# Two batches interleaved at the head of a fused attention and maximum-layer kernel

## The chip, the cores and the metric

The kernel runs on one core of one Trainium2 chip. Its time is the device time of one execution in microseconds. TensorE (PE) multiplies, VectorE (DVE), ScalarE (ACT) and GpSimd (POOL) work on SBUF beside it, and the kernel issues all its DMAs from SyncE (SP). Each engine works through its own list of instructions in order and waits at an instruction until what it needs is there.

## What is computed

A packed attention for each of 8 batches and 8 heads (576 tokens, 64 wide): 32 packed queries p attend to the tokens' k and v, and then the tokens' q attend to the 32 results as keys and values. Behind it, over the 512 columns of all heads, stand two layers: the maximum of three products with 512 x 768 weights, and a product with W_out (768 x 512).

```python
def sm_attn(qq, kk, vv):
    s = scale * np.matmul(qq, kk.transpose(0, 1, 3, 2))
    s = s - np.max(s, axis=-1, keepdims=True)
    a = np.exp(s)
    a = a / (np.sum(a, axis=-1, keepdims=True) + 1e-09)
    return np.matmul(a, vv)
p_packed = sm_attn(p, k, v)
out = sm_attn(q, p_packed, p_packed)
...
h = np.maximum(np.maximum(x @ w1, x @ w2), x @ w3)
return (h @ w_out).astype(np.float32)
```

## The kernel before

**The weights** arrive as 64-bit floats; each of 18 tiles of the first layer (j = 0 to 5, c = 0 to 2; 128 x 512) and 6 of W_out is made 32-bit floats by `to_f32` (L97): two ACT steps (L108, L112), one DVE shift (L114) and one POOL add (L118). W_out's tiles are then split in a rounded part (hi) and a rest (lo), L90. Tiles of j = 0 and 1 land in the buffers with the tag "h", the others in four slots of `stage`.

**A batch.** `scores` (L184) multiplies the packed queries with k, takes the maximum on DVE and the exponential on ACT; `turn` (L219) transposes the result on PE; `values` (L238) multiplies with v; `packed` (L258) transposes the result into `pt_sb`. `att2` (L266) multiplies q with it, turns 32 x 32 blocks on DVE, subtracts the maximum on POOL, takes the exponential on ACT, normalizes and turns back on DVE, and splits the weights in hi (ACT) and lo (POOL): `a2h`, `a2l`. `pw_step` (L319) multiplies a weight tile column j with `pt_sb`, so that the layer needs only the 32 packed rows of each head, and splits the product in hi (ACT) and lo (DVE). `moe_in` (L373) forms for each j and half of the tokens (hf) three sums of six products (hi*hi, lo*hi, hi*lo for two groups of heads r) and takes their maximum on ACT and DVE (L399, L402); the hidden tile is split again. `moe_out` (L411) forms eight output blocks (m, hf), each of 6 x 3 products with W_out, copies them on ACT and sends them out on SP.

**The order.** Batch 0's attention is written out as one list (`FIRST`, L42). From then on PE follows a clock: each step of `moe_in` and `moe_out` is one tick (60 per batch), and `STAGES` says at which tick the stages of the next batch's attention and the projections begin; the other engines' order is left to the scheduler. Layer one of batch 0 takes its weights as they are converted (`CONVERT`, L55), layer two follows, and batch 1's attention lies in between these at ticks 10 to 46 (`STAGES_0`). Then comes batch 1, and so on.

PSUM has two double banks (`ps_big`: scores, turned weights, q's scores, projections) and four single ones (`ps_moe`: the layers' sums; batch 0's `turn`). k, v share four buffers (tag "kv"), hidden tiles seven (tag "h").

Of the kernel before, what the change touches and what calls it, by code (L numbers as in the profile page):

```python
# [10 lines left out]
F32 = mybir.dt.float32  # L11
# [11 lines left out]
P = 128  # L23
G = 2
# [37 lines left out]
def fused_kernel(ctx: ExitStack, tc: tile.TileContext, kp, qt, va, vb, wi, wo, out):  # L62

# [24 lines left out]
    stage = const.tile([P, NST * 2 * WC], F32, name="stage")  # L88

    def split(hi, lo, src, eng_hi, eng_lo):  # L90
        if eng_hi is nc.scalar:
            nc.scalar.copy(out=hi, in_=src)  # L92
        else:
            eng_hi.tensor_copy(out=hi, in_=src)
        eng_lo.tensor_tensor(out=lo, in0=src, in1=hi.bitcast(F32), op=ALU.subtract)  # L95

    def to_f32(dst, src, n):  # L97

        words = src.bitcast(U32).rearrange("p (n two) -> p n two", two=2)
        low, high = words[:, :, 0], words[:, :, 1]
        nc.scalar.activation(  # L108
            out=high.bitcast(F32), in_=high.bitcast(F32), func=AF.Prelu, scale=2.0 ** -111, alpha=-2.0 ** 32,
        )  # L110
        up = low.bitcast(I32)
        nc.scalar.activation(out=up, in_=low, func=AF.Copy, scale=2.0 ** -29)  # L112
        yield 1
        nc.vector.tensor_scalar(  # L114
            out=dst.bitcast(U32), in0=high, scalar1=3, scalar2=None, op0=ALU.logical_shift_left,
        )
        yield 1
        nc.gpsimd.tensor_tensor(out=dst.bitcast(I32), in0=dst.bitcast(I32), in1=up, op=ALU.add)  # L118

# [3 lines left out]
    staged = {}  # L123
    slot = [0]

    def next_slot():
        k = slot[0] % NST
        slot[0] += 1
        return stage[:, k * 2 * WC:(k + 1) * 2 * WC].bitcast(I64)

    def load_w_in(j, c):

        if j < 2:
            t = pool.tile([P, WC], I64, name=f"wi{j}_{c}", tag="h", bufs=NJ + 1)
# [5 lines left out]
    def conv(j, c):  # L140
        return to_f32(w_sb[:, j, c * WC:(c + 1) * WC], staged.pop((j, c)), WC)

    def run(stages):
        for _ in stages:
            pass

    def load_w_out(j):
        t = next_slot()
        nc.sync.dma_start(out=t, in_=wo[j])
        staged["o", j] = t  # L150

    def conv_out(j):
        f = pool.tile([P, DM], F32, name=f"wof{j}", tag="t", bufs=4)
        yield from to_f32(f, staged.pop(("o", j)), DM)
        yield 2
        split(wo_hi[:, j], wo_lo[:, j], f, nc.scalar, nc.gpsimd)

    loaded = {}
# [22 lines left out]

    s1, a1, a1t, av, r1, pp = {}, {}, {}, {}, {}, {}

    def scores(b):  # L184

        kt = [loaded.pop(("k", b, g)) for g in range(G)]
        s = [ps_big.tile([P, 2, 512], F32, name=f"s1_{b}_{r}", tag="big") for r in range(R)]
        for hf in range(2):
            for n, (g, pr) in enumerate(QUADS):
                for r in range(R):  # L190
                    o = slice(64 * r, 64 * r + 64)
                    w = 2 * S + 64 * pr + 32 * r
                    nc.tensor.matmul(  # L193
                        out=s[r][32 * n:32 * n + 32, hf, 0:HS],
                        lhsT=kt[g][o, w:w + NP],
                        rhs=kt[g][o, pr * S + hf * HS:pr * S + (hf + 1) * HS],
                        start=True, stop=True,
                    )
        yield 1
        mx = pool.tile([P, R], F32, name=f"mx{b}", tag="mx", bufs=2)  # L200
        nm = pool.tile([P, R], F32, name=f"nm{b}", tag="nm", bufs=2)
        z1 = pool.tile([P, R], F32, name=f"z1_{b}", tag="z1", bufs=2)
        r1[b] = pool.tile([P, R], F32, name=f"r1_{b}", tag="r1", bufs=2)
        for r in range(R):
            nc.vector.tensor_reduce(out=mx[:, r:r + 1], in_=s[r][:, :, 0:HS], axis=AX.XY, op=ALU.max)
# [12 lines left out]

    def turn(b, r):  # L219

# [6 lines left out]
        a = a1.pop((b, r))  # L227
# [10 lines left out]
    def values(b, rs):  # L238
# [25 lines left out]
    a2, last = {}, {}  # L264

    def att2(b):  # L266
        q = [loaded.pop(("q", b, g)) for g in range(G)]
        pt = pt_sb[b % 2]
        s2 = [ps_big.tile([P, 2, 512], F32, name=f"s2_{b}_{r}", tag="big") for r in range(R)]
        for hf in range(2):  # L270
            for n, (g, pr) in enumerate(QUADS):
                for r in range(R):
                    o = slice(64 * r, 64 * r + 64)
                    nc.tensor.matmul(  # L274
                        out=s2[r][32 * n:32 * n + 32, hf, 0:HS],
                        lhsT=pt[o, NP * n:NP * n + NP], rhs=q[g][o, pr, hf * HS:(hf + 1) * HS],
                        start=True, stop=True,
                    )
        yield 2

        e, e3, m2 = [], [], []
        for r in range(R):
            t = pool.tile([P, S], F32, name=f"e{b}_{r}", tag="t", bufs=4)
            for hf in range(2):
                nc.vector.transpose(out=t[:, hf * HS:(hf + 1) * HS], in_=s2[r][:, hf, 0:HS])
# [4 lines left out]
            nc.vector.tensor_reduce(out=m, in_=e3[r], axis=AX.X, op=ALU.max)  # L290
# [5 lines left out]
        for r in range(R):
            nc.scalar.activation(out=e[r], in_=e[r], func=AF.Exp, scale=SCALE)
            yield 1
        for r in range(R):
            z = pool.tile([P, NT], F32, name=f"z2_{b}_{r}", tag="z2", bufs=2)  # L300
            nc.vector.tensor_reduce(out=z, in_=e3[r], axis=AX.X, op=ALU.add)
            nc.vector.tensor_scalar_add(out=z, in0=z, scalar1=1e-9)
            nc.vector.reciprocal(out=z, in_=z)
            nc.vector.tensor_tensor(
                out=e3[r], in0=e3[r], in1=z.unsqueeze(2).to_broadcast([P, NT, NP]), op=ALU.mult,
            )
            yield 1
            et = pool.tile([P, S], F32, name=f"et{b}_{r}", tag="t", bufs=4)
            last["et"] = nc.vector.transpose(out=et, in_=e[r])
            yield 1  # L310
            hi = pool.tile([P, S], F32R, name=f"a2h{b}_{r}", tag="a2h", bufs=4)
            lo = pool.tile([P, S], F32R, name=f"a2l{b}_{r}", tag="a2l", bufs=4)
            split(hi, lo, et, nc.scalar, nc.gpsimd)
            a2[b, r] = (hi, lo)
            yield 1
# [3 lines left out]
    def pw_step(b, j):  # L319
# [256 lines left out]
```

## Time and profile before

| | us |
|---|---|
| median of three runs | 516.0 (515.9 to 517.64) |
| the profiled execution | 517.84 |
| its span | 516.1 |

The span is what the profile sees from the first instruction to the last; an execution lasts 1.74 longer. One execution was profiled. Rows of the profile name the line, the engine, the operation, what it writes and reads by the program's names, the count, the busy time, the mean of one in ns and the idle time of the engine ahead of it, with what ended that idle time. Matmuls overlap their successors, so the time between starts, not a matmul's duration, is what one costs; the chain of work, in which consecutive pieces are merged, gives it.

### The profile page before, as it was taken

Reading aid. Unit: us, or ns where it says so; the run is one execution under the profiler, and the core shown is the slowest. Engines: PE = TensorE matmul, PEld = TensorE weight load, DVE = VectorE, ACT = ScalarE, POOL = GpSimd, SP = SyncE. Lnnn points to the kernel's source line nnn. Section 1 sums busy time; section 2 is a strip of 40 time slices with the busy share of each in tenths; the row PEclk is TensorE's granted clock in tenths of the full one; section 3 lists DMA queues with packets and bytes.
Section 4 is the critical chain, followed back from the end, with each engine's and each line's share of the span. In section 5 each row is a group of like instructions: output and inputs, shape, how many; then the busy total and the mean of one; then the engine's idle time right before and its main releaser. Section 6 shows DMA issues by size and latency. Waiting matters only on the chain.

```text
span 516.1 us, 11443 instructions
## 1 busy us (share of the span) xinstructions
PE 484.8 (94%) x4896; PEld 430.2 (83%) x4896; DVE 237.9 (46%) x470; ACT 203.7 (39%) x410; POOL 138.6 (27%) x108
## 2 busy tenths in 40 slices
PE   5538799899999999999999999999999999999997
PEld 2126588798899888998899888998899888999997
DVE  2494848625381445616381444615381444614420
ACT  4544783324432443424432443424332443423311
POOL 1347769402222122302222122302222122302210
PEclk9558899899999999999999999999999999999999
DMA  8975855012221213212221213212221000010001
GB/s 312 409 256 180 300 196 185 24 69 104 93 93 70 80 47 106 102 70 104 94 93 69 73 56 103 106 70 103 93 93 70 24 2 3 23 70 1 1 24 69
DMA packets 16450, 52.11 MB, mean 101 GB/s; under 512 B 1936, under 2 KB 3216, under 8 KB 16400
## 3 DMA queue, kind: packets, MB, share of 16 engines
q1 hardware_dynamic: 16400, 51.39, 27.8%
q8 instruction: 38, 0.62, 0.5%
q14 instruction: 12, 0.10, 0.1%
HBM read 41.94 MB, written 9.44 MB: 100 GB/s over the span
## 4 chain that ended last, share of the span: by engine, by line
PE 85%; DMA 6%; POOL 3%; DVE 2%; issue 2%; ACT 1%; SPq 1%; POOLq 0%; DVEq 0%; ACTq 0%
PE mi L393 43%; PE mo L427 29%; PE pw L325 6%; DMA stage<-in_wi 4%; PE tp L246 2%; PE s L193 2%; DMA wi<-in_wi 2%; PE s L274 2%; POOL w_sb L118 1%; PE tp L229 1%; DMA stage<-in_wo 1%; POOL wof L118 1%; POOL wo_lo L95 1%; DVE pl L336 1%; POOL e L292 0%
## 5 line engine op out<-in xcount | busy, mean ns | idle before, releaser
L393 PE MATMUL mi<-a2h,ph 128*128 128x288 f32 x576 | 178.4, 310 | 6.8 <-ACT a2h L92 4.9
L393 PE MATMUL mi<-a2l,ph 128*128 128x288 f32 x576 | 171.4, 298 | 3.8 <-POOL a2l L95 3.8
L393 PE MATMUL mi<-a2h,pl 128*128 128x288 f32 x576 | 171.9, 298 | 1.1 <-DVE pl L336 1.1
L427 PE MATMUL mo<-h,wo_hi 128*128 128x288 f32 x768 | 156.5, 297 | 0.0
L393 PEld LDWEIGHTS mi<-a2h,ph 128*128 128x128 f32 x576 | 109.7, 190 | 32.9 <-issue 17.3
L95 POOL TENSOR_TENSOR h<-hf,h 128x576 fp32r<-128x576 f32 x40 | 57.0, 1425 | 271.6 <-ACT h L92 268.4
L427 PEld LDWEIGHTS mo<-h,wo_hi 128*128 128x128 f32 x768 | 125.0, 190 | 0.6 <-issue 0.6
L427 PE MATMUL mo<-h,wo_lo 128*128 128x288 f32 x384 | 114.2, 297 | 1.7 <-POOL wo_lo L95 1.7
L393 PEld LDWEIGHTS mi<-a2l,ph 128*128 128x128 f32 x576 | 109.8, 191 | 4.5 <-POOL a2l L95 4.5
L393 PEld LDWEIGHTS mi<-a2h,pl 128*128 128x128 f32 x576 | 109.9, 191 | 1.7 <-DVE pl L336 1.5
L336 DVE SCALAR_TENSOR_TENSOR pl<-pw,ph 128x768 fp32r<-128x768 f32 x48 | 44.6, 953 | 127.2 <-ACT ph L334 127.2
L399 ACT COPY c<-mi 128x288 f32<-128x288 f32 x96 | 38.0, 396 | 93.3 <-PE mi L393 92.9
L427 PEld LDWEIGHTS mo<-h,wo_lo 128*128 128x128 f32 x384 | 72.7, 189 | 2.0 <-POOL wo_lo L95 2.0
L433 ACT ACTIVATE o<-mo 128x288 f32<-128x288 f32 x64 | 26.3, 411 | 107.7 <-PE mo L427 107.7
L402 DVE TENSOR_TENSOR c<-mi,c 128x288 f32<-128x288 f32 x96 | 43.5, 453 | 54.4 <-PE mi L393 53.5
L402 DVE TENSOR_TENSOR hf<-mi,c 128x288 f32<-128x288 f32 x96 | 43.8, 456 | 27.5 <-PE mi L393 24.1
L92 ACT CAST h<-hf 128x576 fp32r<-128x576 f32 x42 | 28.3, 674 | 43.6 <-DVE hf L402 42.9
L325 PE MATMUL pw<-w_sb,pt 64*32 64x384 f32 x768 | 39.9, 500 | 2.7 <-POOL w_sb L118 1.7
L334 ACT ACTIVATE ph<-pw 128x768 fp32r<-128x768 f32 x48 | 36.6, 807 | 12.7 <-PE pw L325 12.7
L95 POOL TENSOR_TENSOR a2l<-et,a2h 128x576 fp32r<-128x576 f32 x16 | 22.9, 1447 | 39.5 <-ACT a2h L92 34.7
L325 PEld LDWEIGHTS pw<-w_sb,pt 64*32 64x32 f32 x768 | 11.5, 107 | 16.3 <-issue 13.3
L292 POOL TENSOR_TENSOR e<-e,m 128x576 f32<-128x576 f32 x16 | 18.5, 1174 | 18.1 <-DVE m L290 18.1
(64 smaller groups left out, 332.9 us busy)
## 6 DMA issues: line engine op xcount, KB each, us to landing
kt<-in_kp SPq DMA_DIRECT2D x16, 640.0 KB, 5.1
q<-in_qt SPq DMA_DIRECT2D x16, 576.0 KB, 4.8
out_t<-o SPq DMA_DIRECT2D x31, 288.0 KB, 2.1
v<-in_va SPq DMA_DIRECT2D x16, 512.0 KB, 4.8
stage<-in_wi SPq DMA_DIRECT2D x12, 512.0 KB, 4.3
wi<-in_wi SPq DMA_DIRECT2D x6, 512.0 KB, 9.3
stage<-in_wo SPq DMA_DIRECT2D x6, 512.0 KB, 4.7
v<-in_vb SPq DMA_DIRECT2D x16, 64.0 KB, 4.3
```

The costliest lines, as they stand in the source:

```text
L92: nc.scalar.copy(out=hi, in_=src)
L95: eng_lo.tensor_tensor(out=lo, in0=src, in1=hi.bitcast(F32), op=ALU.subtract)
L118: nc.gpsimd.tensor_tensor(out=dst.bitcast(I32), in0=dst.bitcast(I32), in1=up, op=ALU.add)
L292: nc.gpsimd.tensor_tensor(out=e3[r], in0=e3[r], in1=m2[r].unsqueeze(2).to_broadcast([P, NT, NP]), op=ALU.subtract,)
L325: nc.tensor.matmul(out=ps[NP * n:NP * n + NP, r, 0:NW * P], lhsT=pt_sb[b % 2][o, NP * n:NP * n + NP], rhs=w_sb[o, j, n * NW * P:(n + 1) * ...
L334: nc.scalar.activation(out=hi, in_=ps[:, :, 0:NW * P], func=AF.Copy, scale=2.0 ** -WS)
L336: nc.vector.scalar_tensor_tensor(out=lo, in0=ps[:, :, 0:NW * P], scalar=2.0 ** -WS, in1=hi.bitcast(F32), op0=ALU.mult, op1=ALU.subtract,)
L393: nc.tensor.matmul(out=ps[x][:, 0:HS], lhsT=w[:, r, x * P:(x + 1) * P], rhs=a[:, c], start=(r == 0 and n == 0), stop=(r == R - 1 and n == 2),)
L399: nc.scalar.copy(out=c1, in_=ps[0][:, 0:HS])
L402: nc.vector.tensor_tensor(out=dst, in0=ps[x][:, 0:HS], in1=c1, op=ALU.max)
L427: nc.tensor.matmul(out=t[m, hf][:, 0:HS], lhsT=w[:, j, x], rhs=a[:, c], start=(j == 0 and i == 0), stop=(j == NJ - 1 and i == 2),)
L433: nc.scalar.activation(out=o[m][:, c], in_=t.pop((m, hf))[:, 0:HS], func=AF.Copy, scale=2.0 ** -WS)
```

## The change

The first part of the program, up to the end of batch 1, is now one list, `START`, for all engines, PE and SP too. Each word runs the next piece of one stage: a kind, its batch and its indices, and perhaps the engine (v DVE, g POOL, a ACT) for that piece. Lower case k, v, q, w are loads (w6x are W_out's).

| word | stage | its pieces |
|---|---|---|
| S b | scores | PE |
| A b r | weigh and turn | DVE maximum, ACT exp, PE transposes, ACT copies |
| Z b r | invert | DVE reciprocal |
| V b r.., K b, Q b | values, packed, queries | PE, then DVE; PE, then ACT; PE (batch 0 in two halves) |
| B b r (hf) | attend | DVE turn, DVE maximum, subtract (POOL), ACT exp, DVE sum, ACT add, DVE reciprocal, multiply (DVE), DVE turn, hi (ACT), lo (POOL) |
| C j c | convert | ACT, ACT, DVE, POOL; for j = 6 (W_out) also hi (ACT), lo (POOL) |
| P b j | project | PE, ACT hi, DVE lo |
| N b j | layer_in | six pieces on PE, six matmuls each |
| E b j hf | maximum | ACT, DVE, DVE |
| H b j | halves | hi (ACT), lo (POOL; DVE for j = 5) |
| O b | layer_out | 24 pieces on PE, six matmuls each |
| F b k | finish | ACT copy, output DMA |

In the list batch 1's attention comes while batch 0 is in layer one (S1 stands behind N00's first piece, B11 and B10 beside N02). Then the order of layer one is j = 0, 1, 2 of batch 0; 0, 1 of batch 1; 3, 4 of batch 0; 2 of batch 1; 5 of batch 0; 3 of batch 1; O0 follows, then j = 4, 5 of batch 1, and O1, with batch 2's attention beside it. The six tiles of W_out are converted last, from N03 on. Their buffers are k's and v's ("kv"), their float form takes an output buffer ("o"). q of batch 0 is loaded in halves, the first ones ahead of w01 and w02, and v ahead of w00. Batch 0's second softmax runs in halves of 288 columns. Three hidden tiles (`EXTRA`) take slots of "stage", since two batches' don't fit in "h".

From batch 2 on the clock drives as before, with `STAGES` alone; the two groups r of a batch's second softmax are now stages of their own, begun a tick apart, and the small add ahead of its reciprocal is on ACT. `FIRST`, `LOADS`, `STAGES_0`, `CONVERT` and the rule that conversions come behind batch 0's last `et` (`behind`) are gone.

```diff
+START = """
+k00 k01 v00 v01 w00 q000 q010 w01 w02 q001 q011 w10 w11 w12 S0 w20 w21 w22 k10 A00 k11 w30 A01 A00 A01
+A00 Z00 C00 Z01 A01 A00 A01 V00 C01 V01 V00 C01 v10 C02 V01 C01 v11 K0 C02 C01 K0 C00 Q0 C02 Q0 C00 B000
+C02 C10 B000 C10 B000v C11 C00 B001 B000 B010 C11 B000 B010 P00 B000 C12 B000 B010g C12 B000v B010 B000
+B001 B000 B011 P00 B001g B000v B001 B011 C20 B010 B011g C20 B001 P00 B011 B001 B010 B011 N00 C22 B010
+B001 B010g B011 C22 B001v C21 S1 B011 B001 B011g C21 C10 B001 C30 C12 B010 C10 C30 B011 A10 B010 B010g
+B011 A10 C11 N00 C12 N00 B001v E000 A11 B011g C11 E000 A11 E000 N00 C20 P01 Z11 C20 Z10 A10 P01 N00 w31
+C22 A10 P01 C22 N00 A11 E001 C21 N01 E001 C21 A11 E001 N01 E010 C31 V101 w32 C30 q10 E010 C30 C31 q11
+w40 H00a N01 V101 w41 H00g K1 P02 E010 K1 C32 C31 N01 P02 C31 N01 P02 E011 C32 N01 w42 E011 Q1 C32 E011
+C32 H01a N02 B11 C40 w50 H01g N02 C40 B11 N02 E020 B10 B11g C41 N02 C41 B10 P10 B11 B10v E021 N02 B11
+B10 P11 E020 B11 P10 B11 B10 B11g N02 C42 E020 B10 P11 B10 B11 B10g C42 P10 B11 B10 P03 C50 B11g E021
+B10 E021 P03 B10v C50 P11 N10 H02a C42 N10 E100 C40 N10 P03 C42 N10 E100 C40 E100 N10 E101 N10 E101 w51
...
+H12a C63v N05 E050 C62v N05 E051 E050 H12g N05 E050 E051 N13 C65 E051 C65 N13 E130 H05a N13 E130 C65a
+H05v N13 E130 C65g N13 E131 N13 C64 O0 E131 C64 E131 O0 H13a O0 v20 C64v v21 C64v O0 q20 q21 H13g O0 O0
+F00 O0 F01 O0 O0 O0 F02 O0 O0 O0 F03 O0 O0 O0 F04 O0 O0 P14 F05 O0 P14 O0 P14 O0 O0 F06 O0 O0 N14 F07
...
+O1 B20 B21 O1 B20 B21v O1 F15 B20 B21 O1 B20 B21 O1 B20 B21 O1 B20v F16 P20 B21 B20 B21g O1 B20 B21 P20 O1 B20g
...
+"""
+EXTRA = "12 05 13"
...
+STAGES = "P1:0 P2:0 S:6 k:9 P3:12 P4:12 A:17 V:21 v:23 K:24 P5:26 P6:26 Q:31 q:33"
...
+        words = staged.pop((j, c)).bitcast(U32).rearrange("p (n two) -> p n two", two=2)
...
+        yield 1
+        nc.gpsimd.tensor_tensor(out=dst.bitcast(I32), in0=dst.bitcast(I32), in1=up, op=ALU.add)
+        if j == NJ:
+            yield 2
+            split_hi(wo_hi[:, c], dst)
+            yield 1
+            split_lo(wo_lo[:, c], dst, wo_hi[:, c])
...
+    def attend(b, r, hf=None):
+
+        parts = range(2) if hf is None else (hf,)
+        n = HS * len(parts)
+        c = slice(parts[0] * HS, parts[0] * HS + n)
+        nt = n // NP
...
+        on("g").tensor_tensor(out=e3, in0=e3, in1=m.unsqueeze(2).to_broadcast([P, nt, NP]), op=ALU.subtract)
         yield 2
...
+        nc.scalar.activation(out=e, in_=e, func=AF.Exp, scale=SCALE)
+        yield 1
+        z = pool.tile([P, nt], F32, name=f"z2_{b}_{r}_{c.start}", tag="z2", bufs=4)
+        nc.vector.tensor_reduce(out=z, in_=e3, axis=AX.X, op=ALU.add)
+        yield 0
+        nc.scalar.activation(out=z, in_=z, func=AF.Copy, bias=1e-9)
+        yield 0
+        nc.vector.reciprocal(out=z, in_=z)
+        yield 0
+        on("v").tensor_tensor(out=e3, in0=e3, in1=z.unsqueeze(2).to_broadcast([P, nt, NP]), op=ALU.mult)
+        yield 1
+        et = buffer("et", "t", 4)
+        nc.vector.transpose(out=et, in_=e)
+        yield 1
+        hi = buffer("a2h", "a2h", 4, F32R)
+        split_hi(hi, et)
+        yield 0
+        lo = buffer("a2l", "a2l", 4, F32R)
+        split_lo(lo, et, hi)
...
+    with tc.manual_schedule():
+        for word in START.split():
+            name = word.rstrip("vga")
+            chosen[0] = word[len(name):] or None
+            kind, x = name[0], [int(i) for i in name[1:]]
+            if kind == "I":
+                keep_warm(x[0])
+            elif kind in loads:
+                loads[kind](*x)
+            else:
+                if name not in begun:
+                    begun[name] = stages[kind](*x)
+                next(begun[name], None)
```

More of the change, by code (lines that the diff above doesn't have):

```diff
@@ L86, in fused_kernel @@
     pt_sb = [const.tile([P, P], F32, name=f"pt{i}") for i in range(2)]
[L88 to L118, printed above, removed]
@@ L138, in load_w_in @@
         staged[j, c] = t
[L140 to L156, printed above, removed]
@@ L296, in att2 @@
[L296 to L315, printed above, removed]
+            if b == 0 or hf == 1:
+                yield 0
@@ L403, in moe_in @@
[L403 to L417 removed]
+                yield 0
@@ new lines, in maximum @@
+    def maximum(b, j, hf):
+        c = slice(hf * HS, (hf + 1) * HS)
+        c1 = pool.tile([P, HS], F32, name=f"c1_{b}_{j}_{hf}", tag="c1", bufs=2)
+        nc.scalar.copy(out=c1, in_=sums[b, j, hf, 0][:, 0:HS])
+        yield 0
+        if (b, j) not in hidden:
+            hidden[b, j] = pool.tile([P, S], F32, name=f"hf{b}_{j}", tag="h_f", bufs=2)
+        nc.vector.tensor_tensor(out=c1, in0=sums[b, j, hf, 1][:, 0:HS], in1=c1, op=ALU.max)
+        yield 0
+        nc.vector.tensor_tensor(out=hidden[b, j][:, c], in0=sums[b, j, hf, 2][:, 0:HS], in1=c1, op=ALU.max)
@@ new lines, in halves @@
+    def halves(b, j):
+        h = hidden.pop((b, j))
+        if f"{b}{j}" in EXTRA.split():
+            hl = pool.tile([P, 2, S], F32R, name=f"h{b}_{j}", tag="stage", bufs=NST)
+        else:
+            hl = pool.tile([P, 2, S], F32R, name=f"h{b}_{j}", tag="h", bufs=NJ + 1)
+        split_hi(hl[:, 0], h)
+        yield 0
+        split_lo(hl[:, 1], h, hl[:, 0], "v" if j == NJ - 1 else "g")
+        hid[b, j] = hl[:, 0], hl[:, 1]
+    BLOCKS = [(m, hf) for m in range(NM) for hf in range(2)]
@@ L442, in keep_warm, with begin, tick, both @@
             nc.tensor.matmul(out=t[:, 0:P], lhsT=ident, rhs=ident, start=True, stop=True)
-    def load_all(f, b):
-        def stages():
+    stages = {
+        "S": scores, "A": weigh_and_turn, "Z": invert, "V": lambda b, *rs: values(b, rs), "K": packed, "Q": queries,
+        "B": attend, "C": convert, "P": project, "N": layer_in, "E": maximum, "H": halves,
+        "O": layer_out, "F": finish,
+    }
+    loads = {"k": load_k, "v": load_v, "q": load_q, "w": load_w}
+    begun = {}
+    with tc.manual_schedule():
[7 more added lines that the diff above has]
+                loads[kind](*x)
+            else:
+                if name not in begun:
+                    begun[name] = stages[kind](*x)
+                next(begun[name], None)
+    chosen[0] = None
+    clock, due = [0], []
+    def begin(stage, at):
+        due.append([at, len(due), stage])
+    def tick():
+        while True:
+            ready = [d for d in due if d[2] is not None and d[0] <= clock[0]]
+            if not ready:
+                break
+            d = min(ready, key=lambda d: d[:2])
+            wait = next(d[2], None)
+            while wait == 0:
+                wait = next(d[2], None)
+            if wait is None:
+                d[2] = None
+            else:
+                d[0] = clock[0] + wait
+        clock[0] += 1
+    def both(f, b):
+        def steps():
             if b < B:
@@ new lines, in both, with issue @@
+        return steps()
+    def issue(name, b, at):
+        if name in "kvq":
+            begin(both(loads[name], b + 2), at)
+        elif name[0] == "P":
+            j = int(name[1])
+            if b + j // NJ < B:
+                begin(project(b + j // NJ, j % NJ), at)
+        elif b + 1 == B:
+            return
+        elif name == "S":
+            begin(scores(b + 1), at)
+            for r in range(R):
+                begin(weigh(b + 1, r), at + 1)
+                begin(invert(b + 1, r), at + 4)
+        elif name == "A":
+            for r in range(R):
+                begin(turn(b + 1, r), at)
+        elif name == "V":
+            begin(values(b + 1, range(R)), at)
+        elif name == "K":
+            begin(packed(b + 1), at)
+        else:
+            begin(queries(b + 1), at)
+            for r in range(R):
+                begin(attend(b + 1, r), at + 2 + r)
@@ new lines, in fused_kernel @@
+    with tc.manual_schedule(engines={mybir.EngineType.PE}):
+        for b in range(2, B):
+            for x in STAGES.split():
+                name, at = x.split(":")
+                issue(name, b, clock[0] + int(at))
+            for j in range(NJ):
+                products = None
+                for hf in range(2):
+                    e = maximum(b, j, hf)
+                    for i in range(NW):
+                        tick()
+                        if products is None:
+                            products = layer_in(b, j)
+                        next(products)
+                        next(e, None)
+                begin(halves(b, j), clock[0] + 1)
+            products, k = layer_out(b), 0
+            for _, n in THIRDS:
+                tick()
+                next(products)
+                if n == 2:
+                    next(finish(b, k), None)
+                    k += 1
```

333 lines of the change are left out of this document (123 added, 210 removed).

## The prediction

> **What bounds the kernel now.** I read the page's busy lines and slices first, then the chain that ended last.
>
> ```profile
> PE 484.8 (94%) x4896; PEld 430.2 (83%) x4896; DVE 237.9 (46%) x470; ACT 203.7 (39%) x410; POOL 138.6 (27%) x108
> PE   5538799899999999999999999999999999999997
> PEclk9558899899999999999999999999999999999999
> ...
> GB/s 312 409 256 180 300 196 185 24 69 104 93 93 70 80 47 106 102 70 104 94 93 69 73 56 103 106 70 103 93 93 70 24 2 3 23 70 1 1 24 69
> ...
> q<-in_qt SPq DMA_DIRECT2D x16, 576.0 KB, 4.8
> ```
>
> PE is the bound, and it is full from about the eighth slice (100 us) on. All that can be won lies before. The chain, in order of time, gives the price of each piece of PE work and the state at which the two kernels can be compared:
>
> ```profile
> 150.55 19.20 PE mo L427 x144
> 169.75 1.45 PE pw L325 x32
> 171.20 4.97 PE mi L393 x36
> 176.17 1.13 PE s L193 x32
> ...
> 187.88 0.44 PE tp L229 x4
> ...
> 188.87 0.11 PE tp L230
> ...
> 192.16 1.39 PE tp L246 x80
> ...
> 196.12 0.11 PE tp L260
> ...
> 203.44 1.13 PE s L274 x32
> ...
> 208.75 19.20 PE mo L427 x144
> ```
>
> A batch takes 208.75 - 150.55 = 58.2 us. A step of six layer-one products is 4.97/6 = 0.83, one of layer two 19.20/24 = 0.80, a projection 1.45/2 = 0.725, and an attention 1.13 + 2 x (0.44 + 0.11) + 1.39 + 0.11 + 1.13 = 4.9. At 169.75 batches 0 and 1 are done, batch 2's attention too, and batch 2's layers begin. Work on PE up to there: 2 x 58.2 + 4.9 + 0.7 (batch 0's own attention and first projection) = 122.0. So PE has lost 169.75 - 122.0 = **47.75 us**. START ends in this same state (both outputs, A2 to B2, one projection P20), so the question is one number: how much PE loses in START. Behind it both run the same 58.2 per batch.
>
> Next the windows, to see what PE lacks there, and the groups of the first 113 us by form, for durations:
>
> ```profile
> 30.00:40.00 10.00, 5.26 (x17) 4.21 (x18) 9.86 (x12) 2.46 (x5) 7.29 (x6) 0.50 0.47 163
> ...
> 8.00:100.00 92.00, 69.00 (x678) 51.88 (x674) 61.53 (x109) 52.69 (x101) 56.33 (x43) 0.81 0.67 236
> 60.00:93.00 33.00, 31.05 (x345) 26.52 (x343) 23.40 (x45) 20.93 (x42) 26.44 (x20) 1.00 0.57 201
> ```
>
> Columns are window, length, then busy PE, PEld, DVE, ACT, POOL, granted clock, DMA share, GB/s. From 8 to 100 us DVE is busy 61.53 of 92 (67%), POOL 61%, ACT 57%; none is full, each waits for the others while PE waits for all three. At 30 to 40 us DVE is full and the clock is 0.50.
>
> ```profile
> L118 POOL TENSOR_TENSOR w_sb<-w_sb,stage 128x512 int32<-128x512 int32 x12 | 15.9, 1337 | 6.2 <-ACT stage L112 3.2 <-DVE w_sb L114 1.6 <-issue 1.0
> ...
> L108 ACT ACTIVATE stage<-stage 128x512 f32<-128x512 f32 x18 | 12.3, 683 | 11.1 <-DMA stage<-in_wi 9.4 <-DMA stage<-in_wo 1.5
> L112 ACT ACTIVATE stage<-stage 128x512 int32<-128x512 uint32 x18 | 12.1, 673 | 0.0
> L114 DVE TENSOR_SCALAR w_sb<-stage 128x512 uint32<-128x512 uint32 x12 | 11.9, 1015 | 6.5 <-ACT stage L108 6.5
> ...
> L336 DVE SCALAR_TENSOR_TENSOR pl<-pw,ph 128x768 fp32r<-128x768 f32 x7 | 6.7, 951 | 8.4 <-ACT ph L334 8.4
> L334 ACT ACTIVATE ph<-pw 128x768 fp32r<-128x768 f32 x8 | 6.4, 800 | 1.8 <-PE pw L325 1.8
> L95 POOL TENSOR_TENSOR a2l<-et,a2h 128x576 fp32r<-128x576 f32 x4 | 5.8, 1462 | 9.8 <-ACT a2h L92 5.0 <-DVE w_sb L114 4.8
> ...
> L402 DVE TENSOR_TENSOR hf<-mi,c 128x288 f32<-128x288 f32 x12 | 5.5, 455 | 2.8 <-PE mi L393 1.8 <-DVE c L402 0.5
> ...
> L285 DVE STREAM_TRANSPOSE e<-s 128x288 f32<-128x288 f32 x8 | 3.4, 459 | 4.7 <-PE s L274 4.7
> ...
> L114 DVE TENSOR_SCALAR w_sb<-wi 128x512 uint32<-128x512 uint32 x6 | 3.3, 562 | 0.4 <-ACT wi L108 0.4
> ...
> L309 DVE STREAM_TRANSPOSE et<-e 128x576 f32<-128x576 f32 x4 | 3.1, 778 | 0.2
> L304 DVE TENSOR_TENSOR e<-e,z 128x576 f32<-128x576 f32 x4 | 3.0, 754 | 0.1
> L301 DVE TENSOR_REDUCE z<-e 128x18 f32<-128x576 f32 x4 | 2.9, 733 | 2.8 <-ACT e L297 2.8
> ...
> L205 DVE TENSOR_REDUCE mx<-s 128x1 f32<-128x576 f32 x4 | 2.9, 749 | 8.5 <-PE s L193 8.5
> L290 DVE TENSOR_REDUCE m<-e 128x18 f32<-128x576 f32 x4 | 2.9, 742 | 0.1
> ```
>
> **The change part by part.** No work is removed. Until W_out is in use, one weight tile converted costs ACT 0.68 + 0.67, DVE 0.4 to 1.0, POOL 1.34. Before, that buys PE one batch's products (216 x 0.138 = 29.8 for 18 tiles); interleaved, it buys two, and batch 1's attention, which in before stands between the layers with PE short of work, lies beside batch 0's products. PE's work ahead of O0 in the list is 60 steps N (49.8), 10 P (7.3) and two attentions (9.7): 66.8. Behind it are 122.0 - 66.8 = 55.2, so START breaks even with before if O0 starts at 169.75 - 55.2 = **114.5 us**.
>
> DVE ahead of O0: 24 conversion steps at the mean of these rows (0.56 where wi or W_out, 1.015 for stage) 18.9; ten splits of P 9.5; 19 halves of E at 2 x 0.455 17.3; four tiles of B at 2 x 0.459 + 0.742 + 0.733 + 0.778 = 3.17, 12.7; what B's suffix v puts on DVE and its small steps some 5; A, Z, V some 6; lo halves of H and W_out some 4. Sum 73. ACT has 24 x 1.36 + 10 x 0.80 and the copies and exps, about 72. Both are near PE's 66.8: three queues in order, none with much to spare.
>
> So I walk the list, with these rows:
>
> ```profile
> 14.19 0.67 ACT L108 ACTIVATE wi<-wi 128x512 f32<-128x512 f32 x1
> ...
> 19.34 0.66 ACT L108 ACTIVATE wi<-wi 128x512 f32<-128x512 f32 x1 [3.78 <-DMA wi<-in_wi]
> ...
> 20.28 0.85 DVE L285 STREAM_TRANSPOSE e<-s 128x288 f32<-128x288 f32 x2 [4.07 <-PE s L274]
> ...
> 21.89 0.67 ACT L108 ACTIVATE wi<-wi 128x512 f32<-128x512 f32 x1 [1.34 <-DMA wi<-in_wi]
> ...
> 30.31 0.61 PE L393 MATMUL mi<-a2h,ph 128*128 128x288 f32 x1 [4.35 <-ACT a2h L92]
> ```
>
> (1) *Loads.* The first halves of q are moved past w01 and w02 on SP's queue, and v past w00. The bytes ahead of w10 and w11 stay the same, so these come at 19.34 and 21.89 again. w02, before used at 14.19, has two halves of 288 KB more ahead of it, at the 409 GB/s of the page's second slice 1.4 us: 15.6. K0's copy is behind C02 on ACT, so Q0 starts near 17.6 and B000 near 18.8, in place of 20.28.
> (2) *First product.* B000's exp stands on ACT behind C11's first step, which waits for w11: 21.89 + 0.68 = 22.6. From there to P00's split DVE has twelve steps in list order, most of half size, 5.1 us, with two waits: N00 starts at about 28.6 (before: 30.31).
> (3) *Second head pair.* N00's second step needs B010's halves. On ACT six steps of C (C22, C21, C30; 6 x 0.68 = 4.1), B001's hi and a small step stand ahead of B010's hi, from 29.4 on: 34.1, with the hi 34.5. B010's lo on POOL, half of 1.462, ends at 35.2. Then POOL has C12's add, B011's lo and C11's add, 1.34 + 0.73 + 1.34: 38.6, and P01 waits for that last add. Behind it on PE are P01, A10's transposes, two steps N, A11's transposes, 3.5: N01 at 42.1. I add 2.5: A11's transposes need a PSUM buffer which P01's split frees; the clock, 0.50 in this stretch of before, doubles a step's 0.83 for a while; and DVE waits behind POOL (below). N01 at **44.6**, with 13.5 of PE's work done (N00's six steps, two projections, batch 0's attention and half of batch 1's): 31.1 lost. Bounds: 0 to 6 for the 2.5.
> (4) *N01 to N02.* PE has 8.4 in hand and each of the others under 7: nothing lost.
> (5) *Batch 1's softmax.* From Q1 on DVE has 17 list entries to B10's lo half, 12.2 us with four steps of E and one split of P among them. PE has 6 N and 3 P beside them, 7.2: 5.0 lost. Bounds 2 to 10.
> (6) *N10 to O0.* PE 37.8, DVE 27 to 30, ACT 27: a PE short of work only by hiccups. The nearest row is 60 to 93 us of before (PE 31.05 of 33, and busy is not peak): I take 2, bounds 0 to 7. Here W_out is converted. Its loads take the kv buffers, free by then, and k20 behind them on SP waits for the last of these; S2 needs k20 only in O1, 20 us later, so the wait is covered. C64's lo, the last, must come before O0's fifth step.
> (7) *O0 to the end of START.* 55.2 of PE beside some 24 on DVE or ACT: 0 to 2, I take 0.
> (8) *Batches 2 to 7.* Same steps on PE. Attention's slots move by a few of 60, behind PE's cover; before, PE does not wait there at all. Nothing.
>
> Sum: 31.1 + 5.0 + 2 = 38.1 lost in place of 47.75: some **9.5 us less**. O0 starts at 66.8 + 38.1 = 105, START ends at 160.1. The profiled execution took 517.84 (span 516.1); it would take 508.3. Against the median of the three runs, 516.0, the forecast is **506.5**.
>
> One cost in (3) and (5) is open: DVE beside POOL. The answer for line 114 gives durations as min/median/max, and the timeline shows a case:
>
> ```profile
> L114 DVE TENSOR_SCALAR w_sb<-stage x12: 418/1075/1619, 34.2 to 70.4; 128x512 uint32<-128x512 uint32 x12
> ```
>
> The same shape takes 0.42 or 1.6. Nine such steps and four tensor_tensors on DVE lie between N00 and N10, while POOL has hardly a gap there. At 0.6 more for each of the nine and 0.8 for the four (as if each took twice its 0.75) that is 8.6; I took about 2, since the list puts some of these steps where POOL waits. The Trainium skill, SBUF — State Buffer, section "Who interferes with whom", says that a DVE tensor_scalar in a two-port mode, or a DVE operation with two SBUF inputs, and a GpSimd operation exclude each other for a whole instruction. By that rule the trace's spread (0.42 to 1.62, beside adds of 1.34) is as expected, and the full 8.6 would be owed.
>
> **The rivals.**
> *A. The three engines keep up.* For it: ACT, DVE and POOL have 72, 73 and 53 us for 95, and the list mixes them finely. Then only the walk's 42.1 - 13.5 = 28.6 is lost, with 0 to 3 in (5) and (6): 16 to 19 us less, 497 to 500. Against it: from 8 to 100 us none of them reached 70%, and (5) has DVE full by its own sum.
> *B. The shared port at full price.* 8.6 in place of 2 in (3) and (5), the rest as forecast: 2.9 us less, 513.1. For it: the 1.075 median above. Against it: half-size steps hold the port for half as long, and (5)'s subtract and multiply are mostly on POOL itself.
> *C. Slower: the in-order queues stay as leaky as before.* One fixed order on every engine lets one late tile hold up all behind it, on all engines. If DVE reaches only the 67% that it had from 8 to 100 us, its 73 take 109, and O0 starts at 8.5 + 109 = 117.5, 3.0 behind the break-even: 519. It decides from 73/(114.5 - 8.5) = 69% downwards; my forecast is 73/96.5 = 76%. Against it: DVE's idle time in the rows above (8.4 ahead of P's splits, 6.5 ahead of conversions, 4.7 ahead of B) is each time one stream waiting for its own last step, where the list now puts steps of another.
>
> **How the numbers follow.** Forecast (502 to 511) 0.62, A 0.20, B 0.12, C 0.06. About 0.5% (2.6 us) can be told from no change. Faster by more: 0.62 + 0.20 + half of B = 0.87; within it the other half of B and the edge of the forecast, 0.07; slower 0.06. For 8 in 10 I leave out the lower part of A, and C with the worst of B: 499 to 513.
>
> **What would show it.** N00's first product near 28 to 29 us, its second step near 35; N01 at 42 to 46; a gap of some 5 us on PE ahead of N10 with DVE full; O0's first product at 102 to 108; then no wait on PE and 58.2 per batch. If O0 starts before 97, A is right, after 112, B or C; B, if line 114's counterpart is at 1.0 us or more in its median, C, if DVE idles behind ACT or DMA. Batches of other than 58.2 us would refute (8), and a first product after 31 would refute (1) and (2).

## The result, and the profile after

The kernel takes **503.55 us** (median of 4 runs, 503.04 to 504.87) where the kernel before takes 516.12 beside it (515.9 to 517.64): a ratio of **0.975**, 95% interval 0.973 to 0.978. The forecast was 506.5, in a range of 499 to 513. The profiled execution took 503.85 (before 517.84), 14.0 us less; its span is 502.1. The profiled execution of before was 1.7 above its median and that of after 0.3, so the 14.0 between the two traces stand for 12.6 between the medians.

From the page of the kernel after, the busy line and two of the lines of 40 slices (12.55 us each):

```profile
PE 479.2 (95%) x4888; PEld 425.9 (85%) x4888; DVE 237.1 (47%) x483; ACT 209.6 (42%) x437; POOL 129.5 (26%) x104
...
PE   4569899999999999999999999999999999999997
...
PEclk9679899999999999999999999999999999999999
```

PE's work is the same, and its busy time fell by 5.6 us only, while the span fell by 14.0: some 8.4 us of what went is waiting. The first eight slices of PE read 5538 7998 before and 4569 8999 now, and the clock's second to fourth slices, 5, 5, 8 before, are 6, 7, 9.

The chain that ended last (start, length, engine, group), three of its pieces, gives the forecast's common state and the length of a batch:

```profile
155.77 1.45 PE pw L356 x32
...
194.76 19.19 PE mo L434 x144
...
252.94 19.20 PE mo L434 x144
```

The two projections at 155.77 are PE's first work behind START: this is the state that before reached at 169.75. A batch takes 252.94 - 194.76 = 58.2, as before. So the whole difference, 169.75 - 155.77 = 14.0, lies ahead of 155.77, and PE has lost 155.77 - 122.0 = **33.8 us** there in place of 47.75.

The timeline of PE (start, duration, line, operation, and in brackets the idle time ahead of it with what ended it) shows where these 33.8 lie:

```profile
17.48 2.18 PE L295 MATMUL s<-q,pt 64*32 64x288 f32 x32 [1.46 <-ACT pt L285]
...
25.70 0.61 PE L389 MATMUL mi<-a2h,ph 128*128 128x288 f32 x1 [2.41 <-ACT ph L365]
...
27.88 0.61 PE L389 MATMUL mi<-a2h,pl 128*128 128x288 f32 x1 [1.56 <-DVE pl L367]
...
32.55 0.40 PE L389 MATMUL mi<-a2h,ph 128*128 128x288 f32 x1 [0.60 <-ACT a2h L122]
...
33.48 0.40 PE L389 MATMUL mi<-a2l,ph 128*128 128x288 f32 x1 [0.40 <-POOL a2l L127]
...
37.14 0.87 PE L356 MATMUL pw<-w_sb,pt 64*32 64x384 f32 x12 [0.90 <-POOL w_sb L188]
...
40.61 0.38 PE L389 MATMUL mi<-a2h,ph 128*128 128x288 f32 x1
...
49.37 0.40 PE L389 MATMUL mi<-a2h,ph 128*128 128x288 f32 x1
...
58.13 1.42 PE L356 MATMUL pw<-w_sb,pt 64*32 64x384 f32 x16 [1.74 <-DVE pl L367]
...
59.48 0.61 PE L389 MATMUL mi<-a2h,ph 128*128 128x288 f32 x1
...
99.01 0.30 PE L434 MATMUL mo<-h,wo_hi 128*128 128x288 f32 x1
```

These are, in order, Q0, N00's first product, the first that needs P00's split, N00's second step (its hi, then its lo half), P01, N01, N02, the gap ahead of N10 and N10 itself, and O0. N01, N02 and O0 carry no bracket: PE reaches them without a wait. PE's work up to each of them is that of the forecast's walk, so the loss is 40.61 - 13.5 = 27.1 at N01, 27.5 at N02, 30.5 at N10, 99.01 - 66.8 = 32.2 at O0. From N10 on PE has next to no wait, which the windows of the kernel after (window, length, busy PE, PEld, DVE, ACT, POOL, granted clock, DMA share, GB/s) say as well:

```profile
30.00:40.00 10.00, 8.09 (x82) 5.16 (x67) 8.20 (x20) 6.15 (x15) 8.90 (x8) 0.95 0.25 69
...
60.00:99.00 39.00, 38.45 (x316) 34.78 (x315) 27.85 (x51) 25.34 (x48) 25.47 (x19) 0.98 0.46 157
```

From 30 to 40 us PE is busy 8.09 of 10 at a clock of 0.95; before it was 5.26 at 0.50. But 30.5 of the 33.8 are lost ahead of N10 still: the head is shorter, not cured.

### The profile page after: what moved, and what is told of

Its sections match the earlier page's. It is cut to its first block, busy times and chain, and to the rows that moved or that the text cites. A ratio compares the mean times of both kernels' runs of the same rounds, so it can differ in the third digit from the quotient of the medians.

```text
span 502.1 us, 11442 instructions
## 1 busy us (share of the span) xinstructions
PE 479.2 (95%) x4888; PEld 425.9 (85%) x4888; DVE 237.1 (47%) x483; ACT 209.6 (42%) x437; POOL 129.5 (26%) x104
## 4 chain that ended last, share of the span: by engine, by line
PE 87%; DMA 7%; ACT 1%; DVE 1%; POOL 1%; issue 1%; SPq 1%; ACTq 0%; DVEq 0%; POOLq 0%
PE mi L389 44%; PE mo L434 31%; PE pw L356 6%; DMA wi<-in_wi 4%; DMA v<-in_va 2%; PE tp L268 2%; DMA q<-in_qt 2%; PE s L295 1%; PE s L209 1%; PE tp L251 1%; POOL w_sb L188 1%; ACT wi L173 0%; DVE wo_lo L127 0%; PE tp L252 0%; SPq L151 0%
## 5 line engine op out<-in xcount | busy, mean ns | idle before, releaser
L389 PE MATMUL mi<-a2h,ph 128*128 128x288 f32 x576 | 176.6, 307 | 3.6 <-ACT ph L365 2.4
L127 POOL TENSOR_TENSOR h<-hf,h 128x576 fp32r<-128x576 f32 x38 | 54.5, 1435 | 221.5 <-ACT h L122 221.5
L122 ACT CAST h<-hf 128x576 fp32r<-128x576 f32 x48 | 32.3, 673 | 48.0 <-DVE hf L405 47.3
L324 POOL TENSOR_TENSOR e<-e,m 128x576 f32<-128x576 f32 (+1 forms) x15 | 15.7, 1063 | 60.6 <-PE mo L434 45.8
L188 POOL TENSOR_TENSOR w_sb<-w_sb,wi 128x512 int32<-128x512 int32 x18 | 24.4, 1364 | 25.1 <-DMA wi<-in_wi 14.8
L356 PEld LDWEIGHTS pw<-w_sb,pt 64*32 64x32 f32 x768 | 11.1, 106 | 17.1 <-issue 13.1
```

What stands on the lines that cost most here:

```text
L122: e.copy(out=hi, in_=src)
L127: on(default).tensor_tensor(out=lo, in0=src, in1=hi.bitcast(F32), op=ALU.subtract)
L356: nc.tensor.matmul(out=ps[NP * n:NP * n + NP, r, 0:NW * P], lhsT=pt_sb[b % 2][o, NP * n:NP * n + NP], rhs=w_sb[o, j, n * NW * P:(n + 1) * ...
L389: nc.tensor.matmul(out=sums[b, j, hf, x][:, 0:HS], lhsT=w[:, r, x * P:(x + 1) * P], rhs=a[:, c], start=(r == 0 and n == 0), stop=(r == R - ...
```

## The experiments

Two theories of the gain were to be told apart. Mine: PE is fed because batch 1's work fills batch 0's waits, and the order fixed on all engines is needed for it. The rival: one of the two would do alone, or a small part (loads, halves, W_out's place) carries the gain. Ratios are to the kernel before, with 95% intervals. START is written on fewer or more lines in some of these kernels, so their line numbers stand off by two or three.

**The kernel after once more**, as a measure of what repeats.

> The changed kernel again, beside the next ones on the same chip: 503 to 504.5.

503.04 us, 0.974 (0.972 to 0.976). First product, N01, N02, N10 and O0 stand at 25.52, 40.34, 49.15, 58.89 and 97.81, so the milestones up to N10 repeat to 0.6 us, O0 to 1.2, and the time to 0.5.

**Layer one of batch 1 behind O0.** All words P1x, N1x, E1x, H1x leave their places and stand in a row behind batch 0's outputs; batch 1's attention stays where it is, and every engine's order stays fixed.

```diff
-B10 P03 C50 B11g E021 B10 E021 P03 B10v C50 P11 N10 H02a C42 N10 E100 C40 N10 P03 C42 N10 E100 C40 E100 N10
...
+P11 O0 P11 F07 N10 E100 N10 E100 N10 E100 P12 N10 E101 P12 N10 E101 P12 N10 E101 N11 E110 H10a N11 E110 H10g
```

> Layer one of batch 1 (its P, N, E and H words) is taken out of its places among batch 0's and put behind O0; everything else of the list, loads, halves, engines and order of conversions, stays. My theory, that the gain is the other batch's products put where PE waits for weights: O0 then comes some 27 us of PE work earlier in the list while ACT, DVE and POOL still have about 70 us each ahead of it, so O0 starts no sooner than about 88 and PE loses 10 to 15 us more: START ends at 166 to 171, the time 514 to 519, the whole gain gone. The rival, that the gain comes from the one list on all engines, the loads and the half tiles: 503 to 506.

520.56 us, 1.008 (1.006 to 1.009): 17 slower than after, slower than before too. PE in the timeline, the window of 60 to 100 us, and the end of START and a batch's first outputs in the chain:

```profile
59.62 0.61 PE L387 MATMUL mi<-a2h,ph 128*128 128x288 f32 x1 [3.82 <-ACT ph L363]
...
88.12 0.30 PE L432 MATMUL mo<-h,wo_hi 128*128 128x288 f32 x1
...
94.28 0.40 PE L432 MATMUL mo<-h,wo_hi 128*128 128x288 f32 x1 [2.79 <-DVE wo_hi L122]
```

```profile
60.00:100.00 40.00, 31.51 (x191) 27.97 (x191) 19.28 (x34) 19.17 (x36) 21.74 (x16) 0.81 0.55 189
```

```profile
172.91 1.45 PE pw L354 x32
...
211.90 19.19 PE mo L432 x144
```

O0 starts sooner (88.12), but with only one batch's products done: PE waits for a projection's split (3.82) and in O0 for W_out (2.79), and from 60 to 100 us it has 31.51 of busy time where after has 39.45. START ends at 172.91, 17.1 later than in after. PE's loss is 50.9, more than the 47.75 of before. With the rest of the list as it is, the gain hangs on interleaving PE's work; a list without it, tuned anew, was not tried.

**Order fixed on PE and SP alone.** The same list, but DVE, ACT and POOL get their order from the scheduler, as in before.

```diff
-    with tc.manual_schedule():
+    with tc.manual_schedule(engines={mybir.EngineType.PE, mybir.EngineType.SP}):
```

> The list fixes the order on PE and SP alone; on ACT, DVE and POOL the scheduler orders the same pieces. If the fixed order on all engines carries much of the gain: 508 to 514, with the first product or N10 later by 3 us and more. If the interleaving on PE carries it (my theory): 503 to 506.

526.61 us, 1.019 (1.018 to 1.021). Neither number that I had given was near: against this scheduler's order the fixed one is worth 23 us, and without it the interleaved list is the slowest kernel of all. PE's timeline, then DVE's:

```profile
32.12 0.61 PE L387 MATMUL mi<-a2h,ph 128*128 128x288 f32 x1 [7.65 <-ACT a2h L120]
...
67.92 1.53 PE L354 MATMUL pw<-w_sb,pt 64*32 64x384 f32 x16 [3.80 <-DVE pl L365]
...
80.91 0.61 PE L387 MATMUL mi<-a2h,ph 128*128 128x288 f32 x1 [11.45 <-ACT a2h L120]
```

```profile
73.71 0.78 DVE L336 STREAM_TRANSPOSE et<-e 128x576 f32<-128x576 f32 x1
76.30 1.37 DVE L122 CAST wo_hi<-wof 128x512 fp32r<-128x512 f32 x1 [1.81 <-POOL wof L186]
77.70 1.77 DVE L125 TENSOR_TENSOR wo_lo<-wof,wo_hi 128x512 fp32r<-128x512 f32 x1
79.39 0.77 DVE L336 STREAM_TRANSPOSE et<-e 128x576 f32<-128x576 f32 x1
```

N10 starts at 80.91, 21.4 later than in after. Between the two transposes that end batch 1's softmax DVE waits for a tile of W_out and splits it, 4.9 us, while PE waits 11.45 for what stands behind. W_out isn't used before O0, 40 us later.

**The same with W_out's conversions kept back** until batch 1's last transpose is issued, to see how much of the 23 is W_out's place.

```diff
+                if kind == "C" and x[0] == NJ:
+                    with tc.issue_after(last[1, 0].ins):
+                        next(begun[name], None)
+                else:
+                    next(begun[name], None)
```

> As e2 (order fixed on PE and SP alone), but W_out's conversions are kept behind batch 1's last transpose et, as the kernel before kept its conversions behind batch 0's. If e2 lost its time by the scheduler's placing of W_out's conversions among batch 1's softmax (N10 at 80.9 there): N10 back to 62 to 68, 509 to 514. If the order of everything else is as much to blame: over 518.

518.61 us, 1.004 (1.002 to 1.006), as the second expectation had it: W_out's place is 8 of the 23. PE's timeline:

```profile
32.26 0.61 PE L387 MATMUL mi<-a2h,ph 128*128 128x288 f32 x1 [7.65 <-ACT a2h L120]
...
68.11 0.61 PE L387 MATMUL mi<-a2h,ph 128*128 128x288 f32 x1 [3.07 <-ACT a2h L120]
```

The first product is still at 32.26, 6.6 later than in after, and N10 8.6 later. What makes up the other 15 us was not taken apart.

**All engines fixed up to N10, PE and SP alone behind it.** START is cut at its first N10.

```diff
+    cut = words.index("N10")
+    for part, fixed in ((words[:cut], None), (words[cut:], {mybir.EngineType.PE, mybir.EngineType.SP})):
+      with tc.manual_schedule(**({"engines": fixed} if fixed else {})):
```

> The list fixes all engines up to the first N10 (batch 1's softmax and first splits are then issued), and behind it PE and SP alone. Theory: the order on ACT, DVE and POOL matters where these are nearly full and PE has little in hand, that is before N10 (at 59 us); behind it PE has 38 us beside under 30 on each: 503 to 506. The rival, that the fixed order is worth as much behind N10, where W_out is converted: 508 to 516.

517.27 us, 1.001 (0.999 to 1.002); I had expected the fixed head to keep most of the gain. First product, N01 and N02 are after's (25.40, 40.14, 50.19). Then, on PE and on ACT:

```profile
63.47 1.53 PE L354 MATMUL pw<-w_sb,pt 64*32 64x384 f32 x16 [6.27 <-DVE pl L365]
...
67.49 0.61 PE L387 MATMUL mi<-a2h,ph 128*128 128x288 f32 x1 [2.48 <-ACT a2h L120]
```

```profile
61.73 0.68 ACT L176 ACTIVATE wi<-wi 128x512 int32<-128x512 uint32 x1
62.28 0.68 ACT L171 ACTIVATE wo<-wo 128x512 f32<-128x512 f32 x1
62.84 0.67 ACT L176 ACTIVATE wo<-wo 128x512 int32<-128x512 uint32 x1
63.39 0.67 ACT L120 CAST a2h<-et 128x576 fp32r<-128x576 f32 x1
```

The words behind the cut, free to move, slip ahead of it: two steps of W_out, not needed for nearly 50 us, run just ahead of the hi half that N10 waits for. They cost ACT only some 1.1 us. On DVE five shifts of layer one's tiles start between 51.1 and 61.6, beside batch 1's softmax, where in after not one starts between 49.65 and 60. Two of them stand shortly ahead of the split for which PE waits 6.27:

```profile
59.98 1.70 DVE L182 TENSOR_SCALAR w_sb<-wi 128x512 uint32<-128x512 uint32 x2
```

N10 is 8.0 late, and O0, at 111.64, 12.6 late. Here the fixed order paid only as far as it held: letting it go at N10 cost the whole gain. As the freed words reach back ahead of N10, the run doesn't tell what the order behind N10 is worth by itself.

**Head pairs whole.** B000, B001 and B010, B011 become B00 and B01 of full size.

```diff
-Q0 C00 B000 C02 C10 B000 C10 B000v C11
+Q0 C00 B00 C02 C10 B00 C10 B00v C11
...
```

> Batch 0's second softmax runs in whole tiles of 576 columns (words B00 and B01) in place of halves, at the places of the first halves. If the halves bring the first product forward and this lasts: the first product 1 to 2 us later than 25.7 and the time 1 to 3 us longer, 504.5 to 506.5. The rival, that N01 waits for POOL's adds for j = 1 whichever form the softmax has: within 0.7 us of the control.

505.59 us, 0.978 (0.977 to 0.980). The first product is at 28.51 in place of 25.70, N01 at 41.34, O0 at 101.11. The halves are worth 2 to 2.5 us.

**The order of loads of before, q whole.**

```diff
-k00 k01 v00 v01 w00 q000 q010 w01 w02 q001 q011 w10
+k00 k01 w00 v00 v01 w01 w02 q00 q01 w10
```

> The loads of batch 0 in the order of the kernel before (w00 ahead of v, w01 and w02 ahead of a whole q). By step (1) of the prediction w02 is 1.4 us sooner and q later: q's scores start sooner but end when q is there, near 19.5 in place of 19.7; within 1 us of the control. If q in halves is worth more, 505 to 507.

503.13 us, 0.974 (0.972 to 0.975): no change that can be told. Neither the halves of q nor their place on SP's queue is in the 12.6 us.

**W_out sooner.** W_out's tiles 0 to 2 are loaded and converted ahead of the last layer-one tiles (C6x and C5x, w6x and w5x change places, and C60's and C61's two halves move up).

```diff
-B10 P03 C50 B11g E021 B10 E021 P03 B10v C50 P11
+B10 P03 C60 B11g E021 B10 E021 P03 B10v C60 P11
...
-C51 E110 N11 C51 w52 C50 w60 E111 N11 w61 E111 w62 H10g
+C61 E110 N11 C61 w62 C60 w50 E111 C60a N11 C60g w51 E111 w52 H10g
```

> W_out's tiles 0 to 2 are loaded and converted where layer one's tiles of j = 5 were, and those where W_out's were; P05 moves behind them. My theory: in this stretch PE has 36 us beside under 30 on each other engine, so the place of W_out matters little: 502.5 to 506. The rival, that converting it last is worth something of its own: 507 and more, with PE waiting for P05 or N05.

506.44 us, 0.981 (0.978 to 0.983), between the two expectations: "W_out last" is worth some 3 us. PE's timeline shows part of the price, two waits for splits, where in after PE has no wait from 60 to 90 us:

```profile
77.13 0.40 PE L387 MATMUL mi<-a2h,pl 128*128 128x288 f32 x1 [0.59 <-DVE pl L365]
...
83.72 0.40 PE L387 MATMUL mi<-a2h,pl 128*128 128x288 f32 x1 [0.55 <-DVE pl L365]
```

Ahead of the first one ACT had waited 1.62 us for a tile of W_out (at 73.63) and came to that projection's hi half at 75.30 only.

**The price of the weights, in both kernels.** Layer one's conversion loses its two ACT steps and POOL's add; DVE's step stays. First in after, then in before.

```diff
-        nc.scalar.activation(out=up, in_=low, func=AF.Copy, scale=2.0 ** -29)
+        if j == NJ:
+            nc.scalar.activation(out=up, in_=low, func=AF.Copy, scale=2.0 ** -29)
```

> The two ACT steps and the POOL add of all 18 tiles of layer one are left out (the shift on DVE stays), so ACT has 24 us and POOL 25 us less. If weights limit the head in this kernel still: N01 starts at 35 or sooner (now 40.6), N10 loses nothing, 6 to 10 us less, 494 to 498. If batch 0's own attention chain limits it: first product at 24 to 25.7, N01 at 37 to 39, 2 to 4 us less, 499.5 to 502.

```diff
-        up = low.bitcast(I32)
-        nc.scalar.activation(out=up, in_=low, func=AF.Copy, scale=2.0 ** -29)
+        up = low.bitcast(I32)
+        if whole:
+            nc.scalar.activation(out=up, in_=low, func=AF.Copy, scale=2.0 ** -29)
```

> The kernel before, with the two ACT steps and the POOL add of the 18 tiles of layer one left out. If weights are what PE lacks at the head of that kernel (theory): 8 to 14 us less than before, 502 to 508, where the same cut in the changed kernel (e6) gave 3. The rival, that its two attention chains (batch 0's, and batch 1's between the layers) hold PE and the weights are hidden beside them: 3 to 5 us less, 511 to 513.

In after 500.38 us, 0.969 (0.967 to 0.971), some 3 us less than after; in before 506.41, 0.980 (0.978 to 0.982), 10 less than before. So ACT's and POOL's part in converting layer one's weights holds PE up for 10 us in before and for 3 in after, and these 7 are more than half of the 12.6. That the same 18 tiles now feed two batches would explain it; but the fixed order came with the interleaving, and neither was priced by itself in this way. Without this work the first product in after is 2.2 us sooner, N01 2.8 (37.83) and N10 3.1, as the second expectation had it; what remains of the loss, some 30 us, is not layer one's weights on ACT and POOL.

**Two repairs at the head**, from the waits in after's timeline: K0's copy ahead of C02 on ACT (with B000's exp ahead of C11's step), and C11's add ahead of B011's lo on POOL, since P01 waits 0.90 for that add.

```diff
-C01 v10 C02 V01 C01 v11 K0 C02 C01 K0 C00 Q0
+C01 v10 V01 C01 v11 K0 K0 C02 C02 C01 C00 Q0
...
```

> On ACT the copy of K0 goes ahead of C02's two steps, and B000's exp ahead of C11's. If the head's chain runs through these (theory): q's scores start at 16.4 in place of 17.5, the first product 1 us sooner, and the time 0.7 to 1.2 us shorter than the control, as everything behind moves up. The rival, DVE full from 20 to 30 us or the arrival of w10 and w11 sets the pace: no change within 0.4 us.

```diff
-A11 B011g C11 E000 A11 E000 N00
+A11 C11 B011g E000 A11 E000 N00
```

> On POOL the last add for j = 1 (C11) goes ahead of B011's lo, for which PE has no use before N00's fifth step. Theory: P01, which waits 0.9 us for that add and stands ahead of all else on PE, starts 0.8 us sooner, and N01 too (40.6 to 39.8); the time 0.3 to 0.8 us shorter, which the runs can hardly tell. If batch 1's chain behind it holds N10 at 59, nothing.

503.9 us, 0.975 (0.973 to 0.977), and 504.21, 0.975 (0.973 to 0.978): no gain from either. With K0 first, the first product is at 25.06, 0.6 sooner, and N01 at 40.56, where it was: P01 still waits for POOL, 0.92. With the add first, N01 is at 39.79, 0.8 sooner, but N10 at 59.08 against 59.48 and 58.89 in the two executions of after: lost again in the wait for DVE's split ahead of N10 (1.34 us). No version that does the whole work beat the changed kernel by more than repeats.

## Why the prediction was right, step by step

The direction and the mechanism hold: START's loss on PE sets the result, the batches behind it don't differ, and interleaving plus a fixed order shrinks the loss. The forecast had 38.1 lost and 33.8 were: 4.3 too many, which by steps are 4.0 up to N01, -0.4 from there to N02, 2.0 ahead of N10, 0.3 up to O0, and -1.6 behind. Every milestone that I had named as a sign came sooner than stated. Against the profiled executions the forecast of 508.3 was 4.4 too high, against the medians (506.5) 3.0. The smaller miss is luck: the execution of before that I worked from was 1.7 longer than the median, so the loss that I started from was too large by some of that.

- **(1) Loads.** Q0 at 17.48 (forecast 17.6). DVE's transposes of B000, which I had at 18.8, start at 19.76, behind the scores as a whole:

```profile
19.76 0.48 DVE L318 STREAM_TRANSPOSE e<-s 128x288 f32<-128x288 f32 x1 [1.74 <-PE s L295]
```

- **(2) First product.** 28.6 was the time of the split. The first product needs only hi halves and starts at 25.70; the first that needs the split starts at 27.88, 0.7 ahead of the forecast: B000's exp began at 21.62 in place of 22.6. A product "hi by hi" doesn't wait for a lo.
- **(3) Second head pair: the mis-sized step.** 32.55 and 33.48 for hi and lo (34.5, 35.2), P01's last weights at 37.14 (38.6): 1.5 sooner. From there to N01 I had 3.5, and it took 40.61 - 37.14 = 3.5. So **the 2.5 that I added was not owed at all**. Of its three reasons the clock was wrong: it was back at 0.95 from 30 to 40 us, since PE had work there that it lacked before. The other two, the PSUM buffer and DVE behind POOL, made PE wait nowhere from 37.14 to N01. The 1.5 comes in part from adding rows' durations as if one instruction began where the last one ends. ACT's timeline in this stretch:

```profile
28.89 0.67 ACT L173 ACTIVATE wi<-wi 128x512 f32<-128x512 f32 x1
29.45 0.69 ACT L178 ACTIVATE wi<-wi 128x512 int32<-128x512 uint32 x1
30.02 0.43 ACT L122 CAST a2h<-et 128x288 fp32r<-128x288 f32 x1
```

The steps are 0.67 long and start 0.56 apart: six of them cost 3.4, not 4.1. The Trainium skill, ScalarE: Activation LUTs, section "What ACT_TABLE_LOAD costs", says that back-to-back ACTIVATEs overlap by about 93 ns; the 0.11 here agrees.

- **(4)** 0.4 lost in place of 0.
- **(5) Batch 1's softmax.** The mechanism is as foreseen: DVE full, PE short, a gap ahead of N10. DVE's first and last rows of this stretch, from Q1's scores to B10's lo half:

```profile
49.65 0.85 DVE L318 STREAM_TRANSPOSE e<-s 128x288 f32<-128x288 f32 x2 [0.84 <-PE s L295]
...
59.48 0.75 DVE L127 TENSOR_TENSOR a2l<-et,a2h 128x576 fp32r<-128x576 f32 x1
```

It took 59.48 + 0.75 - 49.65 = 10.6 us, not 12.2, and PE lost 3.0, not 5.0. DVE's two tensor_tensors with both inputs in SBUF there (52.86 and 59.48) start when POOL is free and take 0.76 and 0.75.
- **(6)** 1.7 lost (2), and W_out's place was covered: O0 starts without a wait. Some 0.6 of it goes with the slow clock behind P03's wait: in the control, where P03 took 0.88, O0 starts 38.92 behind N10, here 39.53.
- **(7)** 1.6 lost where I had 0. In the chain PE waits for nothing there, so my unit prices are a little low: the chain has three projections that stand alone at 0.81 each, where I took 0.725, and pairs of output steps at 1.79 in place of 1.60.
- **(8)** 58.2 per batch, as forecast.

*Rival A* (all three engines keep up) named a loss of 28.6 and up to 3; the 33.8 lie between it and the forecast. Its sign, O0 before 97, was missed by 2 us. *Rival B* (the shared port at full price) is refuted by the conversion line on DVE, line 184 in after (minimum, median, maximum in ns):

```profile
L184 DVE TENSOR_SCALAR w_sb<-wi x18: 415/418/994, 15.6 to 76.7; 128x512 uint32<-128x512 uint32 x18
```

The median is 418 where 12 of the 18 steps of before had 1075 (those through the buffer stage; the other six had 418). The 994 shows that the long ones are still there, but in the fixed list they are few. W_out's six steps went the other way, from a median of 424 to 744, in a stretch where PE doesn't wait:

```profile
L184 DVE TENSOR_SCALAR wof<-wo x6: 416/744/1293, 77.0 to 97.5; 128x512 uint32<-128x512 uint32 x6
```

All 24 together took 13.9 us of DVE, where before took 18.4 and I had put 18.9. *Rival C* (in-order queues as leaky as before) did not come about, though its threshold was near: from 8 to 99 us DVE is busy 66.16 of 91 (73%; C decided from 69% down), and O0 was early because DVE had less to do than the 73 of the forecast. A queue in which work not yet needed holds up work that is needed shows where the order is not the list's on every engine: N10 is 8 to 21 us late there, and the gain is gone.

Two questions stay open. Only this scheduler's order was seen beside the fixed list, so whether another free order would do as well isn't shown, nor which engine's order matters most. And of the 27 us lost ahead of N01, some 3 are weights on ACT and POOL; how the rest divides into loads and batch 0's own attention was not tried. The loads are a suspect: from 10 to 30 us the DMA share in after is 1.04 and 1.03, at 388 and 410 GB/s, and the chain that ended last leads through DMA from 5.29 to 32.99.

## What to carry to other kernels

Where a weight must be prepared before use, try to feed two independent streams from it before preparing the next: here, with the order fixed as well, its price on PE went from 10 us to 3. Interleaving needed its order on every engine that feeds the bound one, and for the whole stretch: left to the scheduler, the same list lost 23 us, and work not needed for 40 us stood ahead of work that PE waited for. When you forecast a queue, take the distance between starts from the timeline, not the durations, and don't add a reserve for a slow clock to a stretch whose waits the change removes.

## What the runs showed of the hardware

*One shape, two times.* Two tensor_tensors of DVE in after, same shape, both with two inputs, and POOL's subtract beside the second:

```profile
20.77 0.46 DVE L324 TENSOR_TENSOR e<-e,m 128x288 f32<-128x288 f32 x1
...
23.07 0.90 DVE L335 TENSOR_TENSOR e<-e,z 128x288 f32<-128x288 f32 x1
```

```profile
22.98 0.67 POOL L324 TENSOR_TENSOR e<-e,m 128x288 f32<-128x288 f32 x1 [2.56 <-DVE m L322]
```

The one that starts 0.09 behind POOL's takes 0.90 in place of 0.46: 0.44 more, where 0.58 of POOL's instruction was left. The multiplication as such isn't slower: at 576 columns it took 0.754 in before (L304), and the subtraction 0.76 here, at 52.86. The Trainium skill, SBUF — State Buffer, section "Who interferes with whom", has the one that issues second wait for the first to finish; this pair comes near that.

*The length of one gap doesn't decide the clock.* Ahead of P03 PE was idle 1.74 us in the execution above, and P03 then took 1.42 for 16 matmuls. In before PE was idle longer ahead of a product, 1.86 us, and the projection behind it took 0.88, again for 16 matmuls:

```profile
46.73 0.40 PE L393 MATMUL mi<-a2h,ph 128*128 128x288 f32 x1 [1.86 <-ACT ph L334]
...
48.58 0.88 PE L325 MATMUL pw<-w_sb,pt 64*32 64x384 f32 x16
```

The granted clock was 0.92 from 49 to 60 us in after, and 1.00 from 46 to 50 in before. In the control the gap ahead of P03 was 1.43 us, and P03 took 0.88. So a gap of under two microseconds can cost another half microsecond on the next 16 matmuls in one place, and a longer one nothing in another. What decides it was not tried.
